# Chunk 0's attention in float16, one query scale per chunk or batch, scores in pairs, and a rank for every job: a block-sparse attention with a SwiGLU layer

## Chip, cores and metric

The kernel runs on one core of a Trainium2 chip (trn2). The metric is device time in microseconds (us), the median of repeated executions; each time is that of one whole launch.

## What is computed

For each of 4 batches and 8 heads, 768 queries of 64 elements attend to a part of 768 keys, in blocks of 32. A query block sees its neighbours, the first and the last block and three sampled blocks; the first and the last query block see everything. The result goes through a gated layer.

```python
mask = np.abs(blk_i - blk_j) <= 1
mask = mask | (blk_i == 0) | (blk_j == 0) | (blk_i == n_blocks - 1) | (blk_j == n_blocks - 1)
for qb in range(n_blocks):
    for kb in sampled_blocks[qb]:                      # three per query block
        mask[qb*32:(qb+1)*32, kb*32:(kb+1)*32] = True
scores = np.where(mask, q @ k.T / 8, -1e9)             # per batch and head
attn = softmax(scores) @ v
x = attn.transpose(0, 2, 1, 3).reshape(3072, 512)
g = x @ w_gate                                         # 512 x 1536
out = (g * sigmoid(g) * (x @ w_val)) @ w_out           # 1536 x 512
```

All arrays are float32, and so is the result.

## The kernel before

**Chunks.** A batch is cut into two chunks of 384 queries; `ORDER` lists their blocks. Chunks run from 0 to 7. A chunk has three query tiles (four blocks of 32 each). Chunk 0, 2, 4, 6 hold twelve sparse blocks; chunks 1, 3, 5, 7 hold ten and the two full rows (`full_rows`). After a chunk's attention comes its FFN: twelve column groups `f`, each a gate and a value product (L1328 for chunks 1 to 7, L1217 for chunk 0), then the output product (L1374, and L1252 for chunk 0).

**Numbers as pairs.** Except in chunk 0, a float32 operand is scaled by a power of two and split into a high and a low float16 part (`hi_part` on ScalarE, L285; `lo_part` on VectorE, L288). A product is then three float16 products (high-high, high-low, low-high). The scale comes from a norm: squares summed on ScalarE (`sumsq`, L292), summed over partitions by a float32 product with `ones` on TensorE (L360, L383, L462, L769), and a few small steps on VectorE (`pow2`, L278 to L282). Each of the 21 query tiles of chunks 1 to 7 has a scale of its own (`load_q`).

**Chunk 0.** `first_chunk` works in float32, so that nothing has to be scaled first: K is turned by products with an identity matrix (L581), the blocks' sampled keys are copied by GpSimd (L628), scores are float32 products (L652) with a mask product (L661), the probabilities are normalised and turned by a float32 product with a diagonal matrix (L695, its diagonal from L686), and the values multiply them in float32 (L709). Values come straight from `v` in device memory (L634, gathered rows by L637). `ffn_first` is float32 as well.

**Sparse blocks of the other chunks.** VectorE copies the sampled keys into `kring` (L1017), TensorE makes the scores (`scores`, L1041; in chunk 1 `scores_direct`, L1062 with the mask product L1071), VectorE adds the mask and takes the maximum (L1087; L1080 in chunk 1), ScalarE takes the exponential (L1106), both split the probabilities, a DMA transposes them (`pts`, L1131), and TensorE multiplies by the values (L1144). Values are in device memory as float16 pairs (`vd`), and a block's are read by SP (L1025) and gathered by GpSimd (L1028) into `vring`, three deep. A batch's K goes through a DMA transpose into `kst`.

**Weights.** `w1` (24 tiles of 512 KB) and `w_out` (12) arrive as 64-bit integers and are decoded to float32 by VectorE (`to_f32`, L313 to L315), then, beside chunk 1, split (`split_w1`, `split_w2`). Their places (`wst`) are lent to the raw K, V and queries of batch 0 at first, so some decodes wait for those.

**Who sets the order.** Every step is a job with an engine, a cost in us, what it needs, what buffers it takes, and a rank. `Plan.order` plays the jobs through: whenever an engine is free, the ready job of lowest rank goes next. The emitted program keeps each engine's order, and the SP queue's, as planned. Attention of chunk `ci` has rank `10 * ci` and some tenths, its FFN `1000 + 10 * ci`, evacuations -100 (`EVAC`); the chunk-0 steps stand near 0, K's split of batch 0 at `K0 = 1.5`, V's at `V0 = -1.0`, decoding of the weights at 3 and 5. So on TensorE attention goes ahead of the FFN whenever it is ready. `in_turn` keeps the blocks of one stage in their order.

```python
for t in list_:
    ...
    if best is not None and (t.rank, t.no) > (best.rank, best.no):
        continue
    at = self.may_take(t, now)
```

**Buffers that matter below.** Rings: `qk` (scores in PSUM) 2, `pv` 2, `ffn` 4, `e` 3, `pp` 3, `pts` 3, `st` (raw loads) 4, `q` 1, `sq` 1, `xt` 2.

Of the kernel before, what the change touches and what calls it, by code (L numbers as in the profile page):

```python
# [32 lines left out]
K0, V0 = 1.5, -1.0  # L33
# [3 lines left out]

class Task:
    __slots__ = ("eng", "us", "emit", "need", "rank", "take", "dma", "left", "outs", "next", "ready", "end", "no")
# [13 lines left out]
class Plan:  # L53


    def __init__(self):
        self.tasks, self.depth, self.given = [], {}, {}

# [3 lines left out]
    def add(self, eng, us, emit, need=(), rank=0.0, take=(), use=(), dma=None, behind=None):  # L62
        t = Task()
        t.eng, t.us, t.emit, t.rank, t.take, t.dma = eng, us, emit, rank, list(take), dma
# [87 lines left out]
def tile_block_sparse_attn_swiglu(  # L152
# [28 lines left out]
        "q": (big, [P, 1024], F32, 1),  # L181
        "h": (big, [P, 1536], F16, HB),
# [29 lines left out]
    ones = const.tile([P, P], F32, name="ones")  # L212
    nc.vector.memset(ones, 1.0)
# [16 lines left out]
    ident = const.tile([P, P], F32, name="ident")  # L230

    def identity():
        nc.gpsimd.iota(ident.bitcast(I32), pattern=[[1, P]], base=0, channel_multiplier=-1)
        nc.vector.tensor_scalar(ident, ident.bitcast(I32), 0, None, op0=ALU.is_equal)

    def tables():
# [14 lines left out]
        nc.vector.tensor_copy(qf, qi)  # L251
        nc.vector.tensor_copy(rb, tabv)
        nc.vector.memset(dup, 0.0)
        nc.vector.memset(dup[:, 1, 3:4], 1.0)
        nc.vector.memset(dup[:, NB - 2, 7:8], 1.0)
        for j in range(3):
            d_j = dup[:, :, 4 + j]
            nc.vector.tensor_tensor(df, rb[:, :, j], qf, op=ALU.subtract)
            nc.vector.tensor_tensor(df, df, df, op=ALU.mult)
            nc.vector.tensor_scalar(d_j, df, 1.0, None, op0=ALU.is_le)  # L260
            for edge in (0.0, float(NB - 1)):
                nc.vector.scalar_tensor_tensor(d_j, rb[:, :, j], edge, d_j, op0=ALU.is_equal, op1=ALU.max)
            for i in range(j):
                nc.vector.tensor_tensor(df, rb[:, :, j], rb[:, :, i], op=ALU.is_equal)
                nc.vector.tensor_tensor(d_j, d_j, df, op=ALU.max)

        nc.vector.tensor_scalar(dupm, dup, -(2.0 ** 93), None, op0=ALU.mult)

    t_id = add("DVE", 0.8, identity, rank=-300.0)
    t_tab = add("DVE", 10.0, tables, rank=-200.0)  # L270


    def pow2(nrm, s_out, i_out, n, name, less=0):
# [8 lines left out]
        nc.vector.tensor_scalar(i_out.bitcast(I32), ai, 50 << 23, None, op0=ALU.add)  # L282

# [67 lines left out]
    def split_w1(rank):  # L351
        last = [None, None]
        for f2 in range(0, NF, 2):
            r = rank + 0.1 * f2
# [4 lines left out]
            def norm(fs=fs, n=n):  # L359
                nc.tensor.matmul(  # L360
                    get(n, f"nrm_w1_{fs.start}")[:, 0:4], ones, wacc[:, fs, :].rearrange("p f m -> p (f m)"),
                    start=True, stop=True,
                )
# [8 lines left out]
            t = add("PE", 0.5, norm, sq, r, take=[n])  # L372
            t = add("DVE", 0.8, scale, [t], r, use=[n])
# [4 lines left out]
    def split_w2(rank):  # L378
        sq = [square_w(2, f, oacc[:, f : f + 1], rank + 0.01 * f) for f in range(NF)]
        n = Buf("qk")  # L380

        def norm():
            nc.tensor.matmul(get(n, "nrm_w2")[:, 0:NF], ones, oacc, start=True, stop=True)  # L383
# [10 lines left out]
        t = add("PE", 0.5, norm, sq, rank + 0.2, take=[n])  # L394
        t = add("DVE", 1.4, scale, [t, w1_split[-1][0]], rank + 0.2, use=[n])
        last = None
        for f in range(NF):
            last = split_w(2, f, oss[:, f : f + 1], rank + 0.3 + 0.01 * f, [t], last)
# [1061 lines left out]
```

## Time and profile before

| what | before |
| --- | --- |
| time, median of 3 runs | 867.76 us (866.47 to 870.07) |
| the profiled execution, first to last instruction | 874.2 us |
| TensorE busy | 810.1 us, 7590 products |
| VectorE, ScalarE, GpSimd busy | 602.5, 522.0, 179.6 us |
| moved by DMA | 138.13 MB |
| FFN products of chunks 1 to 7 (L1328, L1374) | 344.5 and 170.8 us |
| first FFN product of chunk 0, of chunk 1 | 97.2 us, 233 us |

The profile gives busy time by engine. A group of instructions is listed with its line, engine, operation, names of output and inputs, shapes and count; then its busy time in us, the mean of one in ns, and the engine's idle time just before such instructions with what ended it. PE is TensorE, DVE VectorE, ACT ScalarE, POOL GpSimd, SP the queue that issues most DMAs. A row of the timeline begins with its start and its length in us. A float32 product leaves two records. The profiled execution's only time on record is its span; the median comes from other executions.

### The profile page before, as it was taken

To read this page: it belongs to the slowest core of one execution; us is meant where nothing else is said; L and a number is where in the kernel's file an instruction comes from. 1 tells how busy PE (TensorE), PEld (TensorE's weight loads), DVE (VectorE), ACT (ScalarE), POOL (GpSimd) and SP (SyncE) were. 2 spreads that over 40 slices of the span, in tenths; PEclk is the share of its full clock that TensorE was granted. 3 is DMA by queue.
4 is the path that set the end of the run, shared out by engine and by line. 5 is a ranking of instruction groups with operands and counts; after the bars stand their busy time and mean duration, and the time that the engine had idled before them with its cause. 6 is when DMAs were issued, how large, how long until landed. Compare 5 with 4: busy or idle time off the path is not lost.

```text
span 874.2 us, 20573 instructions
## 1 busy us (share of the span) xinstructions
PE 810.1 (93%) x7590; PEld 487.9 (56%) x7590; DVE 602.5 (69%) x1924; ACT 522.0 (60%) x1274; POOL 179.6 (21%) x221
## 2 busy tenths in 40 slices
PE   4788899988799988889999999999999899999998
PEld 3577655544465545556556555665556456655653
DVE  4799799875678876777378857884588578841220
ACT  2666474677765775677358666895466567741220
POOL 3141100002032221132123211241124112310220
PEclk9599899999799997999999999999999999999999
DMA  9989966269974997596978794878767864830001
GB/s 228 297 260 278 261 126 211 55 126 216 183 202 121 185 233 146 110 163 148 265 161 151 161 190 84 182 174 235 172 143 137 164 167 80 164 79 25 1 1 36
DMA packets 189972, 138.13 MB, mean 158 GB/s; under 512 B 138480, under 2 KB 150896, under 8 KB 189872
## 3 DMA queue, kind: packets, MB, share of 16 engines
q1 hardware_dynamic: 184240, 119.52, 60.7%
q0 software_dynamic: 5632, 17.31, 8.3%
q8 instruction: 59, 0.97, 0.5%
q14 instruction: 41, 0.34, 0.1%
HBM read 80.68 MB, written 12.58 MB: 107 GB/s over the span
## 4 chain that ended last, share of the span: by engine, by line
PE 66%; DMA 19%; DVE 10%; issue 2%; SPq 2%; ACT 1%; DVEq 0%; ACTq 0%
PE p L1328 33%; PE po L1374 14%; DMA pts<-pp 8%; PE p L1217 5%; PE pv L1144 5%; PE qk L1041 3%; DMA ptsf<-ppf 2%; DMA w2raw<-in_w_dram 2%; DMA qraw<-in_q_dram 2%; DVE w L314 2%; DVE w L315 2%; DMA qs<-qraw 2%; PE po L1252 1%; DMA w<-in_v_dram 1%; DMA kraw<-in_k_dram 1%
## 5 line engine op out<-in xcount | busy, mean ns | idle before, releaser
L1328 PE MATMUL p<-xt,w 128*128 128x384 f16 x2016 | 344.5, 328 | 1.6 <-ACT xt L1165 0.8
L1328 PEld LDWEIGHTS <-w 128*128 128x128 f16 x2016 | 192.7, 99 | 134.8 <-issue 14.9
L1374 PE MATMUL po<-w,h 128*128 128x512 f16 x756 | 170.8, 379 | 0.0
L1028 POOL DMA_INDIRECT vring<-vd,vidx x76 | 72.2, 950 | 336.8 <-PE pv L1144 264.9
L1349 POOL TENSOR_TENSOR h<-act,h 128x384 f16<-128x384 f32 x84 | 82.1, 979 | 274.5 <-ACT h L1346 274.0
L1374 PEld LDWEIGHTS <-h 128*128 128x128 f16 x756 | 71.5, 98 | 83.5 <-issue 4.2
L1144 PEld LDWEIGHTS <-vring 128*128 128x128 f16 x1824 | 64.8, 100 | 36.3 <-issue 27.8
L1144 PE MATMUL pv<-pts,vring 128*128 128x64 f16 x1824 | 67.8, 195 | 18.4 <-DMA pts<-pp 18.3
L1335 DVE SCALAR_TENSOR_TENSOR act<-act,p 128x384 f32<-128x384 f32 x84 | 46.2, 550 | 55.6 <-ACT act L1332 54.6
L1106 ACT ACTIVATE e<-e,nb,es 128x256 f32<-128x256 f32 x132 | 78.2, 593 | 2.2
L1332 ACT ACTIVATE act<-p,gsc 128x384 f32<-128x384 f32 x84 | 48.6, 578 | 47.9 <-PE p L1328 38.8
L1346 ACT CAST h<-act 128x384 f16<-128x384 f32 x84 | 42.5, 505 | 54.4 <-DVE act L1338 53.7
L288 DVE SCALAR_TENSOR_TENSOR pp<-e,rr,pp 128x256 f16<-128x256 f32 x152 | 71.7, 513 | 4.4 <-ACT pp L285 3.5
L285 ACT ACTIVATE pp<-e,rr 128x256 f16<-128x256 f32 x152 | 68.1, 497 | 7.8 <-issue 2.3
L1217 PE MATMUL p<-xt,w 128*128 128x384 f32 x192 | 66.9, 502 | 3.1 <-ACT xt L720 3.1
L1338 DVE SCALAR_TENSOR_TENSOR act<-act,hs,p 128x384 f32<-128x384 f32 x84 | 51.3, 611 | 21.3 <-PE p L1328 18.9
L1087 DVE CUSTOM_DVE_ANT_1 e<-qk,msk 128x256 f32<-128x256 f32 x132 | 50.2, 418 | 13.5 <-PE qk L1041 7.6
L1217 PEld LDWEIGHTS p<-xt,w 128*128 128x128 f32 x192 | 36.2, 194 | 27.7 <-ACT xt L720 3.3
L1165 ACT CAST xt<-pv 64x256 f16<-64x256 f32 x76 | 27.8, 365 | 36.7 <-PE pv L1144 36.1
L1017 DVE COPY kring<-kst 128x256 f16 x228 | 47.1, 262 | 2.5 <-PE qk L1041 2.2
L1170 DVE TENSOR_TENSOR xt<-pv,xt 64x256 f16<-64x256 f32 x76 | 31.9, 420 | 21.1 <-ACT xt L1165 13.8
L1266 ACT ACTIVATE ot<-po,oc 128x512 f32<-128x512 f32 x21 | 14.4, 686 | 47.0 <-PE po L1374 43.1
(183 smaller groups left out, 1082.9 us busy)
## 6 DMA issues: line engine op xcount, KB each, us to landing
vring<-vd SPq DMA_DIRECT2D x76, 192.0 KB
w1raw<-in_w_dram SPq DMA_DIRECT2D x24, 512.0 KB
qs<-qraw SPq DMA_DIRECT2D x84, 128.0 KB
w2raw<-in_w_dram SPq DMA_DIRECT2D x12, 512.0 KB
vfull<-vd SPq DMA_DIRECT2D x12, 512.0 KB
qraw<-in_q_dram SPq DMA_DIRECT2D x42, 128.0 KB
out_dram<-ot SPq DMA_DIRECT2D x20, 256.0 KB
vraw<-in_v_dram SPq DMA_DIRECT2D x9, 512.0 KB
```

Of the source, the lines that this page charges most:

```text
L285: nc.scalar.activation(hi, src, AF.Copy, scale=scale)
L288: nc.vector.scalar_tensor_tensor(lo, src, scale, hi, op0=ALU.mult, op1=ALU.subtract)
L1028: nc.gpsimd.indirect_dma_start(vf[0:96, 1, :], None, bt.vd, bass.IndirectOffsetOnAxis(ap=vidx[0:96, qb : qb + 1], axis=0))
L1087: nc.vector.tensor_tensor_reduce(ev[:, g], stv[:, g], o.msk[:, n, :].unsqueeze(2).broadcast_to([P, 8, BLK]), scale=1.0, scalar=-3.0e38, op ...
L1106: nc.scalar.activation(ev[:, g], sv[:, g], AF.Exp, bias=nb_[:, g : g + 1], scale=o.es[:, 0:1], accum_out=c["rs"][:, g : g + 1],)
L1144: nc.tensor.matmul(pvv[:, j, n % 2], vg[:, cc, l, 2 * j : 2 * j + 2, :], pq[:, g, m, cc, u : u + 2, :], start=i == 0, stop=i == 5,)
L1217: nc.tensor.matmul(buf.tile[:, 0:T], wst[m][:, f + 1, k_ * P : (k_ + 1) * P], x_f32()[:, k_, :], start=k_ == 0, stop=k_ == NKT - 1,)
L1328: nc.tensor.matmul(t[:, 0:T], w_[:, f, m, k_, :], xt.tile[:, l, k_, :], start=i == 0, stop=i == 11)
L1332: nc.scalar.activation(get(act, f"act_{ci}_{f}"), pg.tile[:, 0:T], AF.Tanh, scale=c["gsc"][:, f : f + 1])
L1338: nc.vector.scalar_tensor_tensor(act.tile, act.tile, c["hs"][:, 1:2], pw.tile[:, 0:T], op0=ALU.mult, op1=ALU.mult)
L1349: nc.gpsimd.tensor_tensor(hv()[:, 1, :], act.tile, hv()[:, 0, :], op=ALU.subtract)
L1374: nc.tensor.matmul(po.tile, hv[:, l, ts_], wo16[:, f, m, :], start=f == 0 and i == 0, stop=f == NF - 1 and i == 2)
```

## The change

- **Chunk 0's attention** goes through the common `attention` and `block`, in float16 pairs. K and V of batch 0 are therefore loaded, scaled and split first (`K0 = -6`, `V0 = -3`). K isn't transposed by DMA but turned by TensorE with a float16 identity and evacuated by ScalarE and VectorE in turn. The turning of the probabilities by a float32 product with a diagonal stays; its result is now split into a high part (ScalarE) and a low part (VectorE). The key copies stay on GpSimd. Values now go through `vd`, with nine slots in place of three: six lie in the place of `w_out`, whose decodes wait for them. `ffn_first` stays float32.
- **Query scale**: one for chunk 0, one for chunk 1, one for each batch after that (`open_q`). Chunk 0's tiles are kept from the norm to the split; the other 18 tiles are loaded once for the norm and again for the split (`load_q`).
- **Norms** multiply the upper half of each float32 sum, as bfloat16, with a bfloat16 `ones_h` (`col_sums`) instead of float32 with float32.
- **Scores** of two neighbouring sparse blocks are one TensorE job, for chunks 2 to 7. For the full rows, a job does both halves, and products for the two halves of the output's partitions alternate.
- **Tables** on repeated blocks move from VectorE to GpSimd.
- **Ranks**: each job has a key, and a table `SHIFT` of some 350 numbers adds to its rank. Jobs of a rank at or below -50 have no key.

```diff
-K0, V0 = 1.5, -1.0
+K0, V0, TAB = -6.0, -3.0, -2.0
...
+SHIFT = {
+    "a0.0": -105.32, "a0.1": 0.02, "a0.2": -38.31, "a1.0": -72.7, "a1.1": -11.99, "a1.2": -2.34, "a2.0": -13.58, "a2.1":
...
+    -92.77, "b0.1.2": -21.09, "b0.1.3": -98.46, "b0.2.0": -15.5, "b0.2.1": -20.59, "b0.2.2": -185.09, "b0.2.3": -9.36,
...
+    "b7.1.3": -148.58, "b7.2.0": -70.58, "b7.2.1": 2.23, "b7.2.2": 31.04, "b7.2.3": 10.72, "d0.0": -16.53, "d0.1": -60.76,
+    "d0.10": 29.04, "d0.11": -70.48, "d0.2": -12.06, "d0.3": 0.42, "d0.4": -133.78, "d0.5": -0.61, "d0.6": 31.37, "d0.7":
+    -217.44, "d0.8": 18.62, "d0.9": -314.91, "d1.0": -166.8, "d1.1": -19.21, "d1.10": 66.79, "d1.11": 4.22, "d1.2":
+    -436.63, "d1.3": -45.6, "d1.4": -0.52, "d1.5": -224.13, "d1.6": -211.31, "d1.7": -258.75, "d1.8": -11.17, "d1.9":
...
+    -28.35, "f7.2": -57.69, "f7.3": 151.83, "g0": -197.17, "g12": 92.25, "g18": 73.25, "g3": -5.65, "g6": 90.23, "k0":
+    -59.56, "k1": -6, "k2": 4.77, "k3": 90.38, "n2": 41.11, "o0.0": -21.44, "o0.1": 223.87, "o0.2": 105.89, "o1.0": 21.67,
...
+        t.key = self.key if rank > -50.0 else ""
+        t.rank = rank + SHIFT.get(t.key, 0.0)
...
+    def col_sums(dst, acc):
+        top_half = acc.bitcast(BF16).rearrange("p (n two) -> p n two", two=2)[:, :, 1]
+        nc.tensor.matmul(dst, ones_h, top_half, start=True, stop=True)
...
-                need = scores_f32 if f == NF - 1 else ([v0_lo], batches[0].v_done)[m] if f >= 5 else []
+                plan.key = f"d{m}.{f}"
+                need = ([v0_lo], batches[0].v_done)[m] if 5 <= f < NF - 1 else []
...
-            need = [k0_lo] if f < 5 else scores_f32
+            plan.key = f"d2.{f}"
+            need = v_first[RING + (f + 1) // 2] if f < NF - 1 else []
...
+                if here:
+                    for g in range(2):
...
+                                nc.tensor.matmul(kp.tile[:, u * P : (u + 1) * P], src[:, h * P : (h + 1) * P], ident_h, start=True, stop=True)
...
+                        a = add("PE", 0.5, turn_pe, [l_, t_id], rank, take=[kp])
...
+                        done.append(add("DVE" if g else "ACT", 0.7 if g else 0.6, keep, [a], rank, behind=None if f0 else done[0],
...
-    def first_chunk(rank):
...
-    def first_block(qb, sub, n, rank, kT, q, q_there, kept, regs, regbuf, loaded, pv):
...
+    def open_q(tiles, rank):
...
+        at = tiles[0] < NSUB
...
+        for i in range(0, len(tiles), 1 if at else 2):
...
+            t = add("SP", 0.12 * len(some), load, [], rank, take=hold[:1], dma=1.2 * len(some))
+            g.loaded = t
+            sq.append(add("ACT", 0.24 + 0.5 * len(some), square, [t], rank, take=hold[1:], use=hold[:1]))
...
+        need = [g.scaled]
+        if not at:
+            need.append(add("SP", 0.12, load, [], rank, behind=g.loaded, take=hold, dma=1.2))
...
+                for i in range(2):
+                    st = get(qk[i], f"qkf_{b}_{j}_{i}")
                     for l in range(2):
-                        nc.tensor.matmul(
...
+                        for hh in range(2):
+                            nc.tensor.matmul(
...
+                first = [next(x) for x in two]
+                qks = [x[2] for x in first]
+                a = in_turn("qk", "PE", 1.05, lambda first=first: [x[1]() for x in first], [x[0] for x in first] + [o.done], r,
+                            take=qks, use=[o.qs])
...
+        if first:
+            vslot = no % (RING + 6)
...
+        if first:
+            a = in_turn("inv", "DVE", 0.75, inv, [a], rank, take=[dg])
+            a = in_turn("turn", "PE", 1.2, turn_pe, [a, t_id], rank, take=[pt], use=[dg, e])
+            a = in_turn("high", "ACT", 0.65, turned_high, [a], rank, take=[pts], use=[pt])
+            a = in_turn("low", "DVE", 0.75, turned_low, [a], rank, use=[pts, pt])
...
-    first_chunk(0.0)
     load_kv(0, "k", K0, [])
     k0_lo = batches[0].last_lo
+    group = open_q(chunk_tiles(0), K0 - 0.5)
     load_kv(0, "v", V0, [])
     v0_lo = batches[0].last_lo
+    prepare(0, 0.0, group)
...
+    attention(0, 0.0, [qt[s] for s in range(NSUB)])
     decode_w1(W1_DEC)
     decode_w2(W2_DEC)
```

`SHIFT` keys: `a` the key offsets of a query tile, `b` a sparse block, `d` the decode of a weight tile, `f` full rows, `g` and `q` queries, `k` and `v` a batch's keys and values, `n` and `s` norms and splits of the weights, `p` and `o` FFN products.

More of the change, by code (lines that the diff above doesn't have):

```diff
@@ L370, in scale @@
                 )
[L372 to L373 removed]
+            t = add("PE", 0.15, norm, sq + [x[0] for x in w1_split[-1:]], r, take=[n])
+            t = add("DVE", 0.8, scale, [t], EVAC, use=[n])
             for f in (f2, f2 + 1):
@@ L457, in load_kv @@
             sq.append(add("ACT", 1.24, lambda i=i: square(i), [loads[i]], rank, behind=sq[0] if i else None,
-                          take=parts if here and not i else [], use=bufs[i : i + 1] + ([] if here and not i else parts[:1])))
+                          use=bufs[i : i + 1] + parts[:1]))
         n = Buf("qk" if b else "ffn")
         def norm():
-            nc.tensor.matmul(get(n, f"nrm_{what}{b}")[:, 0:3], ones, sc["acc"], start=True, stop=True)
+            col_sums(get(n, f"nrm_{what}{b}")[:, 0:3], sc["acc"])
         def scale():
@@ L759, in two @@
-        def two():
-            return st.tile.bitcast(F16)[:, 1024:2048].rearrange("p (l n) -> p l n", l=2)
-        def square():
-            o.acc = small_t([P, 1], "qacc", f"qacc_{si}")
-            sumsq(st.tile[:, 0:512], o.acc, two()[:, 0, :])
-        n = Buf("qk")
-        def norm():
-            nc.tensor.matmul(get(n, f"nrm_q{si}")[:, 0:1], ones, o.acc, start=True, stop=True)
-        def scale():
-            o.siq = small_t([P, 2], "siq", f"siq_{si}")
-            pow2(n.tile[:, 0:1], o.siq[:, 0:1], o.siq[:, 1:2], 1, f"q{si}")
+                sl, src = q_rows(si, hh)
@@ L913, in full_rows @@
+            pvs.append(in_turn("pv", "PE", 0.9, product, there + vl, rank, take=[] if j else [pv],
+                               use=turned + vbuf + ([pv] if j else [])))
         xs = Buf("xs")
```

581 lines of the change are left out of this document (280 added, 301 removed), and 40 rows, old and new, of the table SHIFT.

## The prediction, made before the changed kernel was run

> **What bounds the kernel now.** I read the page first, then three stretches of the trace, cut at TensorE's first FFN matmul and at the first FFN matmul of chunk 1.
>
> ```profile
> span 874.2 us, 20573 instructions
> ...
> PE 810.1 (93%) x7590; PEld 487.9 (56%) x7590; DVE 602.5 (69%) x1924; ACT 522.0 (60%) x1274; POOL 179.6 (21%) x221
> ...
> PEclk9599899999799997999999999999999999999999
> ```
> ```profile
> 0.00:97.00 97.00, 69.17 (x738) 60.19 (x738) 73.87 (x188) 52.86 (x152) 28.51 (x64) 0.84 0.94 267
> 97.00:233.00 136.00, 123.82 (x985) 69.36 (x986) 108.17 (x306) 88.14 (x206) 6.87 (x7) 0.97 0.75 160
> 233.00:874.00 641.00, 617.09 (x5868) 358.30 (x5866) 420.51 (x1431) 380.99 (x918) 144.19 (x150) 0.99 0.65 141
> 40.00:60.00 20.00, 17.53 (x229) 15.23 (x228) 19.12 (x46) 13.73 (x44) 8.88 (x18) 0.92 0.85 265
> ```
>
> The columns after the length are PE, PEld, DVE, ACT, POOL, clock, DMA share, GB/s. From 97 us on TensorE is the bound: it idles 136 - 123.8 = 12.2 us in the second stretch and 641 - 617.1 = 23.9 us in the third. Before 97 us it isn't: it is 71% busy, while DVE is busy 19.1 of the 20 us from 40 to 60. Whatever shortens the first stretch shortens the run one for one, and behind it a microsecond of TensorE work counts fully. The timeline shows the start of each step in that first stretch:
>
> ```profile
> 32.97 3.68 PE L709 MATMUL pv<-pts,vring 128*128 128x64 f32 x16 [1.20 <-ACT pts L698]
> ...
> 39.83 1.92 PE L695 MATMUL pt<-dg,e 128*128 128x128 f32 x8
> ...
> 45.26 1.11 PE L695 MATMUL pt<-dg,e 128*128 128x128 f32 x8
> ...
> 97.18 4.54 PE L1217 MATMUL p<-xt,w 128*128 128x384 f32 x8 [3.15 <-ACT xt L720]
> ```
> ```profile
> L314 DVE SCALAR_TENSOR_TENSOR w<-w1raw,w 128x512 int32<-128x512 int32 x24 | 16.6, 692 | 0.8
> L315 DVE SCALAR_TENSOR_TENSOR w<-w1raw,w 128x512 int32<-128x512 int32 x24 | 16.6, 692 | 0.8
> L313 DVE TENSOR_SCALAR w<-w1raw 128x512 int32<-128x512 int32 x24 | 10.6, 444 | 2.6 <-DMA w1raw<-in_w_dram 2.6
> L670 DVE TENSOR_REDUCE mx<-qk 128x2 f32<-128x512 f32 x12 | 8.2, 682 | 2.4 <-PE qk L661 2.3
> L686 DVE TENSOR_SCALAR dg<-ident,rr 128x128 f32<-128x128 f32 x24 | 6.0, 290 | 0.4
> L288 DVE SCALAR_TENSOR_TENSOR w<-w,vs,w 128x512 f16<-128x512 f32 x6 | 4.0, 737 | 0.0
> L553 DVE TENSOR_SCALAR rs<-rs 128x2 f32<-128x2 f32 x12 | 2.2, 187 | 0.0
> ...
> L554 DVE RECIPROCAL rr<-rs 128x2 f32<-128x2 f32 x12 | 2.0, 166 | 0.4
> ```
>
> From the first value product at 33 us to the FFN at 97 us the 12 blocks take 64.2 us, 5.35 each. One block costs DVE 0.68 (maximum) + 0.19 + 0.17 (reciprocal) + 2 x 0.29 (diagonals) = 1.62 us, and one decoded weight tile 0.444 + 2 x 0.692 = 1.83 us. With the 24 W1 tiles that is two per block: 1.62 + 3.66 = 5.28. So the first stretch goes at DVE's pace, because the order puts two decodes beside each block. TensorE's float32 products there are covered.
>
> **Part 1: chunk 0 in float16.** The prologue gets longer. Shift plus base gives the ranks: W1 tiles d1.2 (3.2 - 436.6 = -433), d1.0 (-164) and d0.4 (-130) and chunk 0's queries (-204) go onto the SP queue ahead of K (-66).
>
> ```profile
> 1.19 1.45 SPq L564 DMA_DIRECT2D w<-in_k_dram  x3
> 2.69 5.18 SPq L569 DMA_DIRECT2D w<-in_q_dram  x6
> ...
> 24.14 1.86 SPq L320 DMA_DIRECT2D w1raw<-in_w_dram  x4
> ...
> 24.58 0.59 PE L462 MATMUL nrm_v<-vacc,ones 128*128 128x3 f32 x2 [5.80 <-ACT w L292]
> ...
> 25.97 1.95 ACT L285 ACTIVATE w<-w,vs 128x512 f16<-128x512 f32 x3 [0.29 <-DVE vs L281]
> ```
> ```profile
> L292 ACT ACTIVATE w<-w 128x1024 bf16<-128x1024 f32 x3 | 3.2, 1056 | 5.9 <-DMA w<-in_v_dram 5.9
> ```
> ```profile
> 588.24 2.52 DMA qs<-qraw
> ```
> ```profile
> L637 POOL DMA_INDIRECT vring<-in_v_dram,vidx x12 | 11.9, 993 | 35.2 <-PE pv L709 23.2 <-DVE dup L262 6.7 <-DMA w1raw<-in_w_dram 4.7
> L628 POOL COPY kring<-w 128x128 f32 x36 | 11.4, 358 | 17.6 <-PE qk L652 15.3 <-PE qk L661 2.3
> ```
>
> SP issues then take 3 x 0.47 + 5.2 + 1.45 = 8 us before K is out; three weight tiles (1.57 MB), queries (0.79) and K (1.57) are 3.9 MB, at 267 GB/s landed by about 17 us, and with another weight tile V (1.57) by 25. K: last square 1.1, norm to first split 1.4 (24.58 to 25.97), then on DVE 6 low parts at 0.74 and 6 evacuations of turned keys, taken at the 0.68 of the 512-wide PSUM read: 17 + 1.1 + 1.4 + 0.65 (first high part, 1.95 / 3) + 8.5 = 29. Five copies on POOL (a key copy has the bytes of the 0.36 us row and twice its elements: 0.36 to 0.72) let the first scores start at 31 to 33. V: 25 + 1.1 + 1.4, its low parts behind K's on DVE until 34, the store of 1.57 MB 5.9 us, a gather 0.99 to issue and 2.5 to land (the query spread at 588 us in the chain that ended last; of like size): the first value product at about 44, not 33. Its price, 11 us, isn't hidden.
>
> By then three blocks stand in the three transposed-probability buffers. Nine blocks remain. A block now costs DVE 1.62 plus the new low part:
>
> ```profile
> L1231 DVE TENSOR_TENSOR h<-act,p 128x384 f32<-128x384 f32 x12 | 6.6, 552 | 0.2 <-PE p L1217 0.2
> ```
>
> This reads one PSUM operand of 384; 512 columns scale to 0.71, so 2.33 us. What decides is how many decodes lie between blocks. The FFN needs its weights tile by tile, not all 24 at its start, and by the shifts 11 of the 24 rank below -40; four of these lie ahead of the blocks. That leaves about one per block: 2.33 + 1.83 = 4.2. Nine blocks: 38 us, end at 82, with the last evacuation and wait of 4 us (3.15 in the row at 97.18) **FFN start at 86**, 11 us earlier. Bounds: with no decode between, ACT and TensorE pace it at about 2.9: 44 + 26 + 4 = 74. With two, as now: 44 + 9 x 6.0 + 4 = 102. I take one, as the ranks say. The moved table work goes to POOL, which waits for keys then anyway.
>
> TensorE's float16 work is not on this path if its clock holds:
>
> ```profile
> 179.10 0.27 PE L1062 MATMUL qk<-kst,qs 128*32 128x96 f16 x8
> ...
> 179.81 1.88 PE L1252 MATMUL po<-w,h 128*128 128x512 f32 x4
> ```
> ```profile
> 568.01 0.62 PE L1041 MATMUL qk<-kring,qs 128*32 128x256 f16 x16
> 568.57 0.87 PE L1144 MATMUL pv<-pts,vring 128*128 128x64 f16 x24
> 569.28 4.06 PE L1328 MATMUL p<-xt,w 128*128 128x384 f16 x24
> 573.18 0.86 PE L1144 MATMUL pv<-pts,vring 128*128 128x64 f16 x24
> ```
>
> A block is 0.71 (scores) + 1.1 (turn, unchanged) + 0.71 (product) = 2.5 us. At the low clock the turn took 1.92 where it takes 1.11 (39.83, 45.26), so a cold block is about 4.6, just over DVE's 4.2. The Trainium skill (TensorE: Matmul & The Clock Gate, Part 1) states that the array runs at half clock until some 3.4 us of sustained activity. The trace agrees (granted share 0.5 in the second slice), and the rule speaks against this change, which leaves TensorE idle for longer. By it nine cold blocks give 44 + 42 + 4 = 90 and the sum ends 4 us later; I keep 86.
>
> **Part 2: 97 to 233 us.** K and V of batch 0 are ready some 60 us sooner relative to the FFN, so chunk 1's attention can lie inside chunk 0's FFN and not behind it. Of the 12.2 us idle I take back half, 6.5 (bounds: 11 saved, 4 lost, as DVE now has 0.87 of its time asked for: 73.9 + 108.2 + 8 for low parts + 2 of 213 us, less about 6 of table work). Norms as one-pass bfloat16:
>
> ```profile
> L360 PE MATMUL nrm_w<-wacc,ones 128*128 128x4 f32 x10 | 1.8, 249 | 1.2 <-DVE p_w L278 0.8 <-DVE p_q L278 0.3
> ```
> ```profile
> L1144 PE MATMUL pv<-pts,vring 128*128 128x64 f16 x1584 | 58.2, 194 | 9.5 <-DMA pts<-pp 9.3
> ...
> L769 PE MATMUL nrm_q<-qacc,ones 128*128 128x1 f32 x34 | 5.8, 241 | 1.6 <-ACT ef L856 1.6
> ```
>
> Five weight norms fall from 0.36 to about 0.12 each: 1.2 saved. With 0.3 below: -8 in all.
>
> **Part 3: from 233 us.** Query norms: 17 of 0.34 us become 3 of 0.12: -5.4. Pairs: a score block takes 568.57 - 568.01 = 0.56 us; FFN matmuls run 3.90 / 24 / 384 = 0.423 ns per column, so four waves of 256 columns are 0.43 and about 0.12 is getting in and out. 33 pairs save one 0.12 each: -4. The Trainium skill (TensorEngine Tiling, Key Properties) says that changing the tiling mode drains the array, which fits; without it this term is 0 and the sum 4 us more. The added wait: a pair takes both score buffers, with the FFN queued behind it on TensorE. Full rows, reordered:
>
> ```profile
> 161.89 0.50 PE L834 MATMUL qkf<-kst,qs 128*64 128x384 f16 x4
> 162.22 0.23 PE L901 MATMUL pvf<-ptsf,vfull 128*64 128x128 f16 x2
> ```
>
> Four matmuls of 384 columns in 0.33 us is two waves of 0.163: the two halves already run side by side. I give -1 for all (0.3 of it in part 2). The query loads now come twice for 18 tiles (4.7 MB, 36 SP issues of 0.86 by the row at 2.69: 31 us of queue), hidden as long as SP has slack; not hidden, they delay the transposes for which products wait 9.3 us here. Fewer scale steps on DVE work the other way. Of 23.9 us idle I take 4 back, bounds 12 saved and 10 lost. Sum: -5.4 - 4 - 0.6 - 4 = -14.
>
> **Sum:** -11 - 8 - 14 = -33, so 874.2 becomes 841 us. The median of the runs, 867.76, is 0.993 of the profiled span, so the time is **835 us**.
>
> **The rivals.** *Better still*: all good ends, the start at 74 and the idle halved and more: -23 - 12.5 - 22 = -57.5, 817 of span, 811 us. For: 36 us of idle TensorE is there to take. Against: DVE at 0.87. *No earlier start*: two decodes stay beside each block, start at 102: +5 - 3 - 11 = -9, 859 us. For: that is today's order; against: the ranks. *Slower*: the pairs stall TensorE. Each pair must find both buffers empty, which is DVE's two maxima away. From 1.13 us per pair on, 33 pairs eat the 33 us and 4.4 more; at 1.5 us the time is 835 + 50 = 885. Against: an FFN group of 2 us can lie between. *The reordering does nothing* (pairs and rows both 0): 840, inside the forecast.
>
> **How the numbers follow.** Half a per cent (863.4 to 872.1) is about what a measurement can tell from no change. Forecast, 822 to 848: 0.50. Better still, below 822: 0.24. No earlier start, 848 to 863: 0.15. Within 0.5%, mixtures: 0.05. Slower: 0.06. Faster is 0.89. The range 806 to 860 leaves a tenth out on either side.
>
> **What would show it.** First value product near 44 us; first FFN matmul near 86 with one decode per block on DVE; the norm lines at a third; two score blocks of 16 matmuls in about 1.0 us; TensorE idle after the FFN start at 25 us. I am wrong if the start lies at 97 or later, if idle behind it is above 40 us, or if the score lines show waits for DVE.

## The result and the profile after

The changed kernel takes 844.26 us (median of 4 runs, 841.67 to 851.08) beside 868.91 us for the kernel before in the same series: 0.9709 of it, 95% interval 0.967 to 0.9749. The profiled execution spans 843.8 us where the one before spans 874.2. The forecast was 835 us in a range of 806 to 860.

The head of the page after:

```profile
span 843.8 us, 20625 instructions
...
PE 769.2 (91%) x7634; PEld 460.9 (55%) x7634; DVE 592.1 (70%) x1784; ACT 528.4 (63%) x1266; POOL 200.7 (24%) x258
...
PEclk9757999989999999999999999999999999999999
```

TensorE has 40.9 us less to do, and the profiled execution is only 30.4 us shorter. The medians are 24.7 us apart: the profiled execution of the kernel before, 874.2 us, is longer than each of its four timed runs. The three stretches, cut again at TensorE's first FFN product of chunk 0 and of chunk 1; columns as before (length, PE, PEld, DVE, ACT, POOL, clock, DMA share, GB/s):

```profile
0.00:102.46 102.46, 47.06 (x842) 38.79 (x842) 83.20 (x206) 68.67 (x170) 51.16 (x101) 0.80 0.92 262
102.46:231.10 128.64, 122.33 (x966) 68.54 (x967) 108.35 (x293) 85.05 (x201) 7.21 (x8) 0.95 0.83 194
231.10:843.80 612.70, 599.83 (x5828) 353.55 (x5826) 400.57 (x1287) 374.64 (x896) 142.32 (x150) 1.00 0.70 151
```

Against the rows of before (97, 136 and 641 us) the first stretch is 5.5 us longer, the second 7.4 us and the third 28.3 us shorter. In the first, TensorE lost 22 us of work and gained 27.6 us of idle time. In the third it is busy 17.3 us less and idle 11.0 us less (12.9 instead of 23.9). The timeline of the first stretch, TensorE's rows:

```profile
43.01 0.46 PE L1051 MATMUL qk<-kring,qs 128*32 128x160 f16 x8 [9.62 <-POOL kring L1005]
...
75.82 0.24 PE L1051 MATMUL qk<-kst,qs 128*32 128x96 f16 x1 [4.28 <-DMA qs<-qsq]
...
79.36 2.35 PE L1168 MATMUL pv<-pts,vring 128*128 128x64 f16 x48
...
102.46 10.93 PE L1255 MATMUL p<-xt,w 128*128 128x384 f32 x24 [1.04 <-ACT xt L1134]
```

The first block's scores on its sampled keys wait until 43 us for GpSimd's copies, the ninth block's until 75.8 for queries, and the first value product is at 79.4 us instead of 33. The third stretch by lines:

```profile
L1369 PE MATMUL p<-xt,w 128*128 128x384 f16 x2016 | 340.3, 326 | 0.0
...
L1168 PE MATMUL pv<-pts,vring 128*128 128x64 f16 x1584 | 57.2, 193 | 5.4 <-DMA pts<-pp 3.7 <-DMA vring<-vd,vidx 1.7
L1030 PE MATMUL qk<-kring,qs 128*32 128x256 f16 x1056 | 35.3, 274 | 0.3 <-DMA qs<-qraw 0.3
L806 PE MATMUL qkf<-kst,qs 128*64 128x384 f16 x96 | 10.1, 332 | 0.0
...
L351 PE MATMUL nrm_q<-qacc,ones_h 128*128 128x3 bf16 x2 | 0.3, 168 | 0.0
```

The same groups before, in the same stretch (the row of L1144 stands in the prediction):

```profile
L1328 PE MATMUL p<-xt,w 128*128 128x384 f16 x2016 | 344.5, 328 | 1.6 <-ACT xt L1165 0.8 <-DVE xt L1170 0.7
...
L1041 PE MATMUL qk<-kring,qs 128*32 128x256 f16 x1056 | 41.3, 275 | 0.3 <-DVE kring L1019 0.2
L834 PE MATMUL qkf<-kst,qs 128*64 128x384 f16 x96 | 13.2, 357 | 3.8 <-ACT ef L856 3.4 <-DVE p_q L278 0.2
```

Score blocks fell by 6.0 us, query norms by 5.5, full-row scores by 3.1, full-row value products by 3.7 (L901 and L902 before, 19.8 us; L875 after, 16.1), the FFN products by 4.2 (same products, higher clock), and waits of value products for turned probabilities from 9.3 to 3.7 us. A group's busy time overlaps that of its neighbours, so these savings add up to more than the 17.3 us.

### The profile page after: what moved, and what is told of

It reads as the page before. It is cut to its first block, busy times and chain, and to the rows that moved or that the text cites. A ratio compares the mean times of both kernels' runs of the same rounds, so it can differ in the third digit from the quotient of the medians.

```text
span 843.8 us, 20625 instructions
## 1 busy us (share of the span) xinstructions
PE 769.2 (91%) x7634; PEld 460.9 (55%) x7634; DVE 592.1 (70%) x1784; ACT 528.4 (63%) x1266; POOL 200.7 (24%) x258
## 4 chain that ended last, share of the span: by engine, by line
PE 68%; DMA 15%; DVE 7%; ACT 3%; issue 3%; SPq 2%; POOL 1%; DVEq 0%; ACTq 0%; POOLq 0%
PE p L1369 33%; PE po L1416 13%; DMA pts<-pp 6%; PE pv L1168 6%; PE p L1255 5%; PE po L1291 4%; PE qk L1030 3%; DMA w<-vd 2%; DVE w L383 2%; DVE w L384 1%; PE pvf L875 1%; DMA qn<-in_q_dram 1%; DMA kraw<-in_k_dram 1%; PE qkf L806 1%; DMA qs<-qraw 1%
## 5 line engine op out<-in xcount | busy, mean ns | idle before, releaser
L1369 PE MATMUL p<-xt,w 128*128 128x384 f16 x2016 | 340.3, 326 | 0.0
L1390 POOL TENSOR_TENSOR h<-act,h 128x384 f16<-128x384 f32 x84 | 80.0, 953 | 304.4 <-ACT h L1387 304.1
L1016 POOL DMA_INDIRECT vring<-vd,vidx x82 | 78.6, 959 | 280.4 <-PE pv L1168 236.9
L1168 PEld LDWEIGHTS <-vring 128*128 128x128 f16 x1968 | 68.9, 99 | 28.2 <-issue 16.2
L357 DVE SCALAR_TENSOR_TENSOR pp<-e,rr,pp 128x256 f16<-128x256 f32 x152 | 77.7, 552 | 7.5 <-ACT pp L354 6.2
L1168 PE MATMUL pv<-pts,vring 128*128 128x64 f16 x1968 | 72.3, 194 | 11.0 <-DMA pts<-pp 6.3
L1255 PE MATMUL p<-xt,w 128*128 128x384 f32 x192 | 70.1, 520 | 1.3 <-ACT xt L1134 1.0
L1255 PEld LDWEIGHTS p<-xt,w 128*128 128x128 f32 x192 | 37.6, 202 | 27.6 <-issue 5.3
L361 ACT ACTIVATE wsq<-w 128x512 bf16<-128x512 f32 x36 | 22.6, 628 | 25.6 <-DVE w L384 16.4
```

The costliest lines, as they stand in the source:

```text
L357: nc.vector.scalar_tensor_tensor(lo, src, scale, hi, op0=ALU.mult, op1=ALU.subtract)
L1016: nc.gpsimd.indirect_dma_start(vf[0:96, 1, :], None, bt.vd, bass.IndirectOffsetOnAxis(ap=vidx[0:96, qb : qb + 1], axis=0))
L1168: nc.tensor.matmul(pvv[:, j, n % 2], vg[:, cc, l, 2 * j : 2 * j + 2, :], pq[:, g, m, cc, u : u + 2, :], start=i == 0, stop=i == 5,)
L1255: nc.tensor.matmul(buf.tile[:, 0:T], wst[m][:, f + 1, k_ * P : (k_ + 1) * P], x_f32()[:, k_, :], start=k_ == 0, stop=k_ == NKT - 1,)
L1369: nc.tensor.matmul(t[:, 0:T], w_[:, f, m, k_, :], xt.tile[:, l, k_, :], start=i == 0, stop=i == 11)
L1390: nc.gpsimd.tensor_tensor(hv()[:, 1, :], act.tile, hv()[:, 0, :], op=ALU.subtract)
```

## Experiments

Each series has its own runs of the kernel before on its chip; a ratio is to those. "Start" is TensorE's first FFN product of chunk 0, "chunk 1" the first of chunk 1, "rest" what lies behind that, "idle" TensorE's idle time in the rest and "turned" what value products waited there for turned probabilities, all in us from each kernel's trace.

| kernel | ratio (95%) | start | chunk 1 | rest | idle | turned |
| --- | --- | --- | --- | --- | --- | --- |
| before | | 97.2 | 232.6 | 641.6 | 24.1 | 9.3 |
| changed | 0.9709 (0.967 to 0.9749) | 102.5 | 231.1 | 612.7 | 12.9 | 3.7 |
| changed, again | 0.9745 (0.967 to 0.982) | 105.9 | 235.8 | 615.1 | 15.0 | 6.1 |
| chunk 0 in float32, no ranks | 1.0114 (1.0045 to 1.0183) | 97.2 | 234.4 | 637.6 | 29.5 | 18.7 |
| no ranks | 0.9977 (0.9935 to 1.0018) | 96.7 | 230.8 | 641.8 | 29.5 | 21.0 |
| pairs taken apart | 0.9899 (0.9849 to 0.9949) | 104.5 | 230.2 | 627.8 | 18.3 | 8.1 |
| norms in float32 | 0.9859 (0.9802 to 0.9915) | 106.3 | 235.9 | 624.4 | 20.2 | 6.7 |
| ranks to chunk 1, none behind | 1.01 (1.0062 to 1.0137) | 103.8 | 239.8 | 639.0 | 27.9 | 18.8 |
| none to chunk 0's FFN, ranks behind | 0.9805 (0.9721 to 0.9889) | 112.0 | 244.5 | 609.0 | 11.2 | 2.7 |
| the same, queries earlier | 0.994 (0.9905 to 0.9976) | 97.4 | 250.2 | 613.4 | 14.2 | 5.2 |
| value products earlier | 0.9786 (0.9717 to 0.9854) | 107.6 | 236.5 | 614.9 | 14.5 | 5.6 |
| decoding cut short | 0.9707 (0.9656 to 0.9759) | 97.7 | 227.4 | 614.3 | 15.7 | 7.4 |
| no ranks, DMA reckoned at 4 | 0.9825 (0.9785 to 0.9864) | 90.4 | 221.6 | 628.8 | 21.4 | 3.3 |
| that to chunk 1, ranks behind | 1.0054 (1.0023 to 1.0086) | 92.5 | 224.0 | 648.9 | 42.2 | 3.1 |

**1. The parts without float16 in chunk 0 and without ranks** (the kernel before with the new norms, query scale, pairs and full rows; the tables stay on VectorE as well):

```diff
-            nc.tensor.matmul(get(n, f"nrm_{what}{b}")[:, 0:3], ones, sc["acc"], start=True, stop=True)
+            col_sums(get(n, f"nrm_{what}{b}")[:, 0:3], sc["acc"])
...
-    def load_q(si, rank, need):
+    def q_rows(si, hh):
...
+    def open_q(tiles, rank):
```

> The kernel before with every part of the change but two: chunk 0 stays in float32, and no job has a shift. Theory A (behind the FFN's start TensorE counts one for one, and the first stretch isn't touched here): FFN start near 97 us as before, norms -6, pairs -6, rows 0 to -3, so 12 to 15 us less than before, about 855. Theory B (the gain comes from chunk 0 in float16, which makes K and V of batch 0 ready sooner): within 4 us of before, 865 to 872.

**2. All of the change but the ranks:**

```diff
-SHIFT = {
...
-}
+SHIFT = {}
```

> The changed kernel with an empty table of shifts. Theory A (the ranks carry what TensorE's idle time lost, 10.9 us in the last stretch and some in the middle): 10 to 20 us slower than the changed kernel, 855 to 865. Theory B (the ranks only move work about, and cost some in the first stretch, where they hold the first value product back to 79 us): FFN start at 90 to 95 and the same time or less, 835 to 846.

Without ranks the change is worth nothing: 0.9977 with all its parts, 1.0114 without float16 in chunk 0. Neither expectation of experiment 1 came. In experiment 2 theory A had the direction, and the loss against the changed kernel's two ratios is 20 to 23 us where 10 to 20 was expected. The TensorE work was saved all the same; it turned into waiting and a lower clock. The third stretch without ranks and, in float32, without either:

```profile
230.80:872.60 641.80, 612.26 (x5832) 361.36 (x5831) 399.52 (x1319) 381.22 (x903) 146.15 (x150) 0.98 0.73 150
```
```profile
234.40:872.00 637.60, 608.02 (x5832) 360.55 (x5831) 402.29 (x1318) 380.02 (x902) 143.76 (x150) 0.98 0.67 150
```

Both have about 29.5 us idle, more than before, and the granted clock is 0.98 where the changed kernel has 1.00: 612.26 us at 0.98 is 600 at 1.00, the changed kernel's 599.83. So the 29.1 us between no ranks and ranks are 16.7 us of idle time and 12.4 us that go with the lower clock. Where they lie shows in one stretch of equal length, without ranks first, then the changed kernel:

```profile
231.00:495.00 264.00, 244.97 (x2411) 147.24 (x2410) 184.99 (x619) 175.64 (x411) 66.67 (x66) 0.95 0.86 183
...
300.00:350.00 50.00, 35.85 (x465) 22.78 (x461) 33.83 (x135) 34.81 (x91) 12.12 (x12) 0.76 1.04 208
```
```profile
231.00:495.00 264.00, 260.56 (x2697) 155.88 (x2696) 203.08 (x657) 187.46 (x453) 68.91 (x73) 1.00 0.85 191
...
300.00:350.00 50.00, 49.54 (x523) 28.62 (x521) 34.36 (x114) 32.91 (x80) 9.26 (x10) 1.00 0.85 184
```

By 495 us the changed kernel is 286 products ahead. From 300 to 350 us TensorE is idle 14.2 us without ranks and 0.5 with them, and its 35.85 us of work at a clock of 0.76 would be 27.2 at 1.00: 13.7 and 8.6 us, together 22 of the 29.1. The matmul groups of these 50 us, in the same order of kernels:

```profile
L1171 PE MATMUL pv<-pts,vring 128*128 128x64 f16 x281 | 13.0, 214 | 12.2 <-DMA pts<-pp 12.1
L1419 PE MATMUL po<-w,h 128*128 128x512 f16 x36 | 8.3, 379 | 0.0
L1372 PE MATMUL p<-xt,w 128*128 128x384 f16 x24 | 6.3, 422 | 1.2 <-ACT xt L1192 0.8 <-issue 0.4
```
```profile
L1369 PE MATMUL p<-xt,w 128*128 128x384 f16 x138 | 23.5, 326 | 0.0
L1416 PE MATMUL po<-w,h 128*128 128x512 f16 x69 | 15.9, 379 | 0.0
L1168 PE MATMUL pv<-pts,vring 128*128 128x64 f16 x120 | 4.3, 193 | 0.5 <-DMA pts<-pp 0.5
```

And the value products of the 69 us ahead of that, without ranks and with them:

```profile
L1171 PE MATMUL pv<-pts,vring 128*128 128x64 f16 x14 | 0.6, 193 | 0.0
```
```profile
L1168 PE MATMUL pv<-pts,vring 128*128 128x64 f16 x168 | 6.2, 193 | 1.7 <-DMA vring<-vd,vidx 1.7
```

With ranks, 168 value products go out between 231 and 300 us, among chunk 1's FFN, and only 120 from 300 to 350, among 138 gate and value products of the FFN and 69 output products. Without ranks they are 14 and then 281 in a heap, with 24 and 36 FFN products to put between them. There, blocks wait six times, up to 2.6 us each, for transposes, while the DMA engines are full (share 1.04). Full DMA engines alone don't make TensorE wait. In the changed kernel's next 50 us their share is 0.99 too, and TensorE doesn't idle:

```profile
350.00:400.00 50.00, 50.00 (x520) 30.09 (x519) 40.62 (x142) 41.35 (x99) 13.06 (x14) 1.00 0.99 205
```

**3. Pairs taken apart, 4. norms in float32**, both in the changed kernel's own order. For the first, the next TensorE job goes out between the two halves:

```diff
     for t in plan.order():
...
+        if hasattr(t, "halves"):
+            give()
+            t.halves[0]()
+            second[0], held[0] = t.halves[1], t
+            continue
         t.emit()
+        if t.eng == "PE":
+            give()
```
```diff
-        top_half = acc.bitcast(BF16).rearrange("p (n two) -> p n two", two=2)[:, :, 1]
-        nc.tensor.matmul(dst, ones_h, top_half, start=True, stop=True)
+        nc.tensor.matmul(dst, ones, acc, start=True, stop=True)
```

> The changed kernel, its planned order kept; only, the second half of each of the 33 score pairs is issued behind the next TensorE job. Theory A (TensorE counts one for one, and going in and out of the narrow tiling costs 0.12 to 0.18 us a time): 4 to 6 us slower, about 849. Theory B (hidden in TensorE's idle time): within 1.5 us of the changed kernel. The score line should go back from 35.3 to about 41 us busy in both.

> The changed kernel, its planned order kept; only, the norms are products of float32 ones with the float32 sums again. 17 norms, of which 15 lie behind the FFN's start: 0.34 instead of 0.17 us. Theory A (TensorE counts one for one): 2 to 4 us slower, about 847. Theory B (norms hide in idle time): within 1 us. Most of the change's saving on norms is then their smaller number (41 to 17), not their type.

The score line of the rest with the pairs apart:

```profile
L1031 PE MATMUL qk<-kring,qs 128*32 128x256 f16 x1056 | 41.8, 275 | 1.0 <-DMA qs<-qraw 0.9
```

41.8 us instead of 35.3 is 0.20 us for each of 33 pairs, where 0.12 was forecast. The starts in the timeline show where it lies, first with the pairs apart, then in the changed kernel:

```profile
541.12 0.62 PE L1031 MATMUL qk<-kring,qs 128*32 128x256 f16 x16
541.67 2.12 PE L1370 MATMUL p<-xt,w 128*128 128x384 f16 x12
543.72 0.62 PE L1031 MATMUL qk<-kring,qs 128*32 128x256 f16 x16
...
556.36 2.11 PE L1370 MATMUL p<-xt,w 128*128 128x384 f16 x12
558.31 0.86 PE L1169 MATMUL pv<-pts,vring 128*128 128x64 f16 x24
```
```profile
543.59 1.06 PE L1030 MATMUL qk<-kring,qs 128*32 128x256 f16 x32
544.58 2.12 PE L1369 MATMUL p<-xt,w 128*128 128x384 f16 x12
```

From start to start a block alone takes 0.55 us and a pair 0.99, 0.11 less than two. Twelve FFN products take 2.05 us ahead of a score block and 1.95 ahead of a value product, so each block apart holds up the products ahead of it by another 0.10. The Trainium skill (TensorEngine Tiling, Key Properties) says that a change of the tiling mode drains the array. The rows agree. As a whole, both kernels come out above the changed one's two ratios: by 1.5 to 1.9% without the pairs (13 to 17 us) and by 1.1 to 1.5% with the old norms (10 to 13 us). These come from different series, and for the norms the interval overlaps that of the changed kernel's second one, so only the order of size is shown. It is more than either expectation had (4 to 6 us for the pairs, 2 to 4 for the norms) and more than the 6.5 us of scores: the rest is 12.7 to 15.1 us longer without the pairs, part of it idle time. Taken apart, the second half's scores also reach VectorE later; what that costs wasn't separated from TensorE's work. So with this order a saving on TensorE shows in the time, by more than its size, and why by more stays open; in experiments 1 and 2 it didn't show at all.

**5. The changed kernel again, 6. no ranks to chunk 0's first FFN product and ranks behind it, 7. ranks to chunk 1's first FFN product and none behind it.** The planned orders of two kernels are cut at that product and joined; jobs already out are skipped.

```diff
-    for t in plan.order():
-        t.emit()
+    by_no = {t.no: t for t in plan.order()}
+    for no in SPLICED.split():
+        by_no[int(no)].emit()
```

> The changed kernel once more, for the measure of the other three on this chip and at this time. 0.97 of the kernel before; FFN start of chunk 0 at 102 to 103 us, chunk 1's FFN at 231, 613 us behind it.

> The changed kernel in a spliced order: up to chunk 0's first FFN product the order that its planner gives with all ranks' shifts at zero, behind it the order with the shifts (jobs already emitted left out). Nothing else differs. Theory A, the shifts pay through the slack that they leave between turned probabilities and value products behind 231 us, and cost 6 us ahead of the first FFN product: the FFN starts at 97, 613 us lie behind chunk 1's start, waits of value products for turned probabilities stay below 7 us in all, and the time is 5 to 6 us under the changed kernel (0.993 of it). Rival B, the shifts pay by the weight tiles decoded and norms done early (20 tiles decoded before the FFN instead of fewer): then the FFN starts at 97 but stage 2 or 3 grows by what was moved, and the time is that of the changed kernel or up to 10 us above.

> The mirror image: the changed kernel's own order up to chunk 1's first FFN product (231 us), and from there the order that the planner gives with the shifts at zero. Theory A: 231 us up to there as in the changed kernel, then 640 us with 20 us of waits of value products for turned probabilities, as with no shifts at all; 870 us, the whole gain gone. Rival B, the gain was prepared ahead of 231 us: the rest takes 613 to 620 us and the time is within 7 us of the changed kernel.

The changed kernel, run again, starts its FFN at 105.9 us instead of 102.5 and has a rest of 615.1 instead of 612.7: differences of 3 us in the table are no more than one kernel shows. With everything up to chunk 1 as in the changed kernel and only the order behind it without ranks, the gain is gone: 1.01. Its rest, and its value products from 300 to 350 us:

```profile
239.80:878.80 639.00, 611.05 (x5827) 360.54 (x5826) 390.86 (x1287) 371.52 (x886) 143.84 (x150) 0.98 0.71 143
```
```profile
L1280 PE MATMUL pv<-pts,vring 128*128 128x64 f16 x288 | 13.7, 216 | 10.1 <-DMA pts<-pp 10.1
```

The heap is back, at the same place. One wait of 5.7 us for V's norm also lies there and may be the joint's; without it the rest would still be 18 to 21 us longer than with ranks. Its chunk 1 also starts later, at 239.8 us. This speaks against the rival that the gain had been prepared ahead of 231 us. The opposite joint has the shortest rest of all (609.0 us) but missed its start of 97 us, by a wait that the joint itself made:

```profile
109.36 0.50 PE L918 MATMUL qkf<-kst,qs 128*64 128x384 f16 x1 [16.34 <-DMA qs<-qraw]
```

A full-row block of chunk 1 stands ahead of the FFN, and its queries went out late behind weight loads.

**8. Value products earlier in stage 1**, in the changed order: the third tile's queries behind the fourth block's scores, the first tile's value products ahead of the ninth block's.

```diff
+    move([at("q2", "spread", "SP")], seq[seq.index(at("b0.0.3", "scores_direct", "PE")) + 1])
+    x = at("b0.2.0", "scores_direct", "PE")
+    late = [t for t in seq[seq.index(x) :] if t.key.startswith("b0.0.")]
+    move(late, x)
```

> The changed kernel with its order edited by hand in stage 1 alone: the four DMAs of the third query tile go out on SyncE right behind the fourth block's scores, and all value products of the first query tile stand ahead of the ninth block's scores on TensorE. Theory Q, stage 1 is held by the order on SyncE and TensorE (value products at 79.4 us stand behind scores whose queries landed at 76.8): value products start by 68 us, the FFN starts at 92 to 97, and the time falls by as much (835 to 840). Rival D, VectorE paces stage 1 (83 of 102 us busy, 20 weight tiles decoded): value products start early but the FFN still starts at 100 to 103, time as the changed kernel within 2 us.

```profile
73.54 2.26 PE L1168 MATMUL pv<-pts,vring 128*128 128x64 f16 x72
...
107.64 7.60 PE L1255 MATMUL p<-xt,w 128*128 128x384 f32 x15 [1.04 <-ACT xt L1134]
```

The products start 7 us earlier than in the changed kernel of this series (80.7), and the FFN doesn't (107.6 beside 105.9). It gained 7 us of the 11 to 13 that theory Q wanted there, and none of them at the FFN, so that wait alone isn't what holds the start.

**9. Experiment 6 mended**: that block's queries scaled and sent five groups of loads earlier, its scores behind six FFN products. **10. Decoding cut short. 11. No ranks, with one number of the planner raised.**

```diff
-        nc.vector.scalar_tensor_tensor(d, hi, -(1 << 30), d, op0=ALU.bitwise_and, op1=ALU.bitwise_or)
-        nc.vector.scalar_tensor_tensor(d, lo, 29, d, op0=ALU.logical_shift_right, op1=ALU.bitwise_or)
```
```diff
-DMA_US = 2.0
+DMA_US = 4.0
...
+SHIFT = {}
```

> The spliced order again (no shifts up to chunk 0's first FFN product, with shifts behind), with what held st1_off_rest_on put right by hand: there a full-row block of chunk 1 stood on TensorE ahead of the first FFN product, and its queries were sent out at 106 us only, behind weight loads; here the queries' scaling and DMAs go out five groups of loads earlier and that block's scores stand behind six FFN products. Theory A (the shifts pay through the order behind 231 us alone): FFN start at 95 to 98, 130 to 134 us of stage 2, 609 to 615 us of stage 3; 0.960 to 0.968 of the kernel before, 5 to 10 us under the changed kernel's ratio of 0.971 to 0.975. Rival: what stage 1 of the changed kernel prepares (20 weight tiles decoded) is missing behind it: stage 2 takes 137 us or more, or stage 3 620 and more, and the ratio is 0.973 to 0.98.

> The changed kernel in its own order with the second and third VectorE operation of each weight tile's decoding left out (part of the decoding, so that W comes out wrong): 1.4 us of VectorE work less for each tile, some 27 us of the 83 in stage 1. Theory D (VectorE, with the 20 tiles that the order decodes ahead of the FFN, paces stage 1): the FFN starts 8 us or more sooner than the changed kernel's 102.5 and 105.9, at 92 to 97. Rival (the order on SyncE, the gathered values and the DMA queue pace it): start at 100 to 106.

> The changed kernel with all shifts at zero and one number of the planner raised, the time that it reckons for a DMA's landing, from 2 to 4: nothing that runs is changed but the order. By the planner's costs 19 of the 76 transposed blocks have less than 4 us of TensorE work between the issue of their transpose and their value product with the shifts at zero, 7 with the shifts, 9 here. Theory A (what the shifts give behind 231 us is this slack): waits of value products for turned probabilities of 10 us or less in stage 3, granted clock 0.99 to 1.00 there, 613 to 625 us. Rival (the shifts act through something else): 635 us and more, as with no shifts. Stage 1 isn't what is asked here.

The mended joint starts its FFN at 97.4 us and has a rest of 613.4, as theory A wanted, but 152.8 us between. That is the rival's longer stage 2, and at 0.994 the kernel is slower than either expectation had. 19.4 us are one wait:

```profile
128.37 1.50 PE L918 MATMUL qkf<-kst,qs 128*64 128x384 f16 x8 [19.40 <-ACT ef L940]
```

Again it stands where the edited block is, so it says more of the joint than of the ranks. Without decoding's second and third operation VectorE has 26.0 to 26.3 us less to do in stage 1 than in the changed kernel's two executions:

```profile
0.00:97.70 97.70, 44.30 (x842) 36.66 (x842) 57.21 (x168) 67.76 (x171) 44.48 (x101) 0.84 0.95 275
```

The start moved by 4.8 to 8.2 us, to 97.7. VectorE is part of what holds it and not all. The kernel without ranks that reckons a DMA's landing at 4:

```profile
0.00:90.40 90.40, 46.60 (x836) 37.52 (x836) 70.98 (x184) 63.15 (x156) 47.41 (x101) 0.84 0.87 253
...
221.60:850.40 628.80, 607.45 (x5832) 359.33 (x5831) 397.71 (x1315) 378.29 (x899) 143.88 (x150) 0.98 0.71 152
```

Here waits for turned probabilities fall from 21.0 to 3.3 us, as the slack said, and the rest from 641.8 to 628.8. That is 13 of the 29 us, and lies between the two expectations. The other 16 are 8.5 us more idle time than in the changed kernel (full-row scores wait 5.6 us for queries and 3.3 for ScalarE) and 7.6 us of busy time at a clock of 0.98. So slack for the transposes is one part of what the ranks do, at most about half: with that number the whole order was planned anew, so not all of the 13 us need be the slack's. This kernel also has the earliest start, 90.4 us, with 13 weight tiles decoded by then.

**12. That order up to the fifth group of chunk 1's FFN, the changed kernel's behind it** (joined as above):

> One more spliced order: up to the fifth group of chunk 1's FFN products the order of off_dma4 (no shifts, a DMA's landing reckoned with 4), which reached chunk 1's FFN at 221.6 us where the changed kernel needs 231 to 236; behind it the changed kernel's own order. 45 jobs that the changed kernel had done by there are still to do, batch 1's keys among them (14 us of ScalarE and 16 us of VectorE by the planner's costs, 1.2 us of TensorE). Theory A (what the shifts buy lies in the order behind 231 us, what they cost lies ahead of it, and the two can be had apart): FFN start at 90 to 93, chunk 1's at 222 to 225, 613 to 622 us behind it, 835 to 845 us in all, 0.962 to 0.972 of the kernel before. Rival B (the later start of the changed kernel is what its later part needs: keys and weights ready early): the 45 jobs hold TensorE up by 10 us and more, 625 us and more behind 222, 0.974 and above.

```profile
251.00 0.16 PE L463 MATMUL nrm_k<-kacc,ones_h 128*128 128x3 bf16 x1 [8.36 <-ACT k L473]
269.35 0.37 PE L1142 MATMUL qk<-kring,qs 128*32 128x256 f16 x1 [18.19 <-DMA qs<-qraw]
```

The 7 to 12 us that it is ahead of the changed kernel at chunk 1 are lost, and 22 to 29 more: chunk 2's keys and queries, which the changed kernel has ready by then, come late. Behind that it has few waits (3.1 us for turned probabilities). Rival B holds here. No version that computes everything beat the changed kernel.

## Why the prediction was right, and where it was not

**Start of the FFN: wrong.** Step "about one decode per block, first value product at 44, start at 86" failed, by 16.5 us; its own rival "no earlier start" had 102. What was read as eleven tiles ahead of the FFN was twenty:

```profile
L384 DVE SCALAR_TENSOR_TENSOR w<-w1raw,w 128x512 int32<-128x512 int32 x17 | 12.1, 714 | 0.6
...
L384 DVE SCALAR_TENSOR_TENSOR w<-w2raw,w 128x512 int32<-128x512 int32 x3 | 2.1, 692 | 0.1
```

The ranks below -40 were counted; a job with a higher rank goes out too when nothing better is ready. The value products weren't paced by the blocks either: in the order they stand behind the ninth block's scores and start at 79.4 us, and 23 us lie between them and the FFN where 42 were reckoned. The same parts in another order start at 96.7 (no ranks) and 90.4 us (13 tiles). From that last one to the changed kernel VectorE has 12.2 us more to do and the start is 12.1 later, which fits its pace; but experiment 10 took 26 us away for 4.8 to 8.2, and what holds the start at 97.7 there stays open. The prediction named a start at 97 or later as the sign of being wrong, and that sign came. TensorE's cold clock (0.80 in the changed kernel's row) wasn't tried by itself. With the pairs apart, in the same order up to here, the clock was 0.93 and the start at 104.5 us, no earlier than in the changed kernel's two executions (102.5 and 105.9); but the turning products weren't shorter there (333 ns on average, beside 329), so this doesn't settle it.

**Stage 2: right.** -7.4 measured, -8 forecast: idle time fell from 12.2 to 6.3 us (6.5 were to be taken back) and busy time by 1.5.

**From 233 us: right in kind, half the size.** -28.3 measured, -14 forecast. Query norms -5.5 (forecast -5.4), though one takes 0.17 us and not 0.12. Pairs -6.0 (-4, and the rival without a mode switch gave 0): the term had the 0.12 us of a block's own and left out the 0.10 by which the products ahead of it are held. Full-row scores -3.1 and their value products -3.7, where -0.6 was put for all of the full rows: the step "the two halves already run side by side" saw one group of four. That eight in one job also save the getting in and out is likely for the scores; no run takes the full rows apart. The FFN products' higher clock, -4.2, had no term. Idle time -11.0 where -4 was taken back, near the bound of 12. That term was the most mis-sized one, and it is the one the ranks make: without them idle is 29.5 us, above the 24.1 of before.

**The rivals.** The pairs don't stall TensorE: the score line waits 0.3 us in all. "Better still" needed a start at 74. Of "no earlier start" the start came but not the 859 us, since it reckoned with 14 us of gain behind it where 35.7 came.

**The sum** came out near, -33 against -30.4 in the profiled executions and -24.7 in the medians, by luck: an error of 16.5 us in one stretch was met by one of 14.3 in the other. "A microsecond of TensorE work counts fully" behind 97 us holds only in an order where nothing else is late: in experiment 1 the rest is busy 9.5 us less than before and only 4 us shorter, and the whole was 1.1% slower by its ratio (its profiled execution, 872.0 us, was the fastest of four).

**What is settled and what isn't.** Shown: the gain needs the ranks, and what they add lies in the order behind 231 us, most of it from 300 to 350 us. Shown in part: up to about half of that goes through slack for the transposes. Not tried: ranks in the kernel before, without the other parts. Not settled: whether the later start is the price of the later gain. Three joints that tried to have both ran into waits at the joint (for queries, for ScalarE's work on a full-row block, for keys and queries), and a joint free of that wasn't found.

## What to carry to other kernels

Before a saving on the busiest engine is counted one for one, look for the stretch where that engine waits in a row for short transfers: without ranks the changed kernel had 28.7 us less TensorE work than before (781.4 of 810.1 us) and the same time, most of it lost where value products came in a heap. Such a stretch was found here by windows of 50 us, not by sums over the run. None of the four orders joined from two halves was faster than the order made as a whole: at three of the joints, one half lacked what the other had ready.

## What the hardware showed besides

In these rows the time of a copy on GpSimd depends on what VectorE does beside it. The same key copy of 128x256 float16, first beside a VectorE cast out of PSUM, then beside a two-input operation on SBUF, and VectorE's first decode step beside these copies:

```profile
26.50 0.39 POOL L1002 COPY kring<-kst 128x256 f16<-128x256 f16 x1 [2.27 <-ACT w L354]
...
36.09 0.85 POOL L1002 COPY kring<-kst 128x256 f16<-128x256 f16 x1
```
```profile
29.99 0.41 DVE L382 TENSOR_SCALAR w<-w1raw 128x512 int32<-128x512 int32 x1
...
37.40 0.62 DVE L382 TENSOR_SCALAR w<-w1raw 128x512 int32<-128x512 int32 x1
```

0.39 us becomes 0.85, and 0.41 becomes 0.62 on the other side: copies on GpSimd cost VectorE time as well. The Trainium skill (GPSIMD Engine Reference, Key points) says that GpSimd shares its SBUF interfaces with VectorE, in conflict with operations of two SBUF inputs; the copies agree.

The clock fell to 0.76 from 300 to 350 us without ranks although no wait there is longer than 2.6 us. The Trainium skill (TensorE: Matmul & The Clock Gate, Part 1) puts the clock to how busy the array has lately been, over a window of about 3.4 us; many short waits were enough here. That the clock alone, without the waits, costs the 12 us was not tried.
